# The subtraction behind a weight's low part, on GpSimd for every second piece of the first layer's weights

## The chip, the cores and the metric

The kernel runs on one core of a Trainium2 chip. A time is the device time of one execution in microseconds (us), measured on the chip; of several runs the median is given. Beside the times stands one execution that the hardware profiler recorded. The engines are TensorE (PE in the profile, PEld its weight loads), VectorE (DVE), ScalarE (ACT), GpSimd (POOL) and SyncE (SP), which issues most transfers.

## What is computed

Attention with a memory term (4 batches, 8 heads, 576 positions, 64 wide), then two feed-forward layers over 2304 tokens (512 wide, 2048 hidden). The reference, cut:

```python
scores = scale * np.matmul(q, k.transpose(0, 1, 3, 2))       # causal mask
a = softmax(scores); local = np.matmul(a, v)
q_p = phi(q)                                                   # elu + 1
mem_out = einsum(q_p, M_prev) / (einsum(q_p, z_prev) + 1e-6)
x = g * mem_out + (1 - g) * local                              # g = sigmoid(beta)
h = x @ w_in1;  r = max(h, 0);  x = (s * r * r + b) @ w_out1   # layer 1
h = x @ w_in2;  x = (h * tanh(softplus(h))) @ w_out2           # layer 2
```

## The kernel before

Every product of the two layers is made in three parts from operands that are split in two: a high part, rounded to the type that TensorE multiplies, and a low part, which is the operand less its high part. The weights come from memory as 64-bit floats, read as pairs of 32-bit words, and are turned into 32-bit floats and split on the chip.

`convert` (line 659) does this for one piece of 128 x 512 numbers. Layer 1 has 32 pieces: for each of four quarters r, four pieces j = 0 to 3 of `w_in1` and four of `w_out1` (lines 1122 and 1131). The steps of a piece, with the profile's lines:

- 673: a transfer of 512 KB brings the words (SP's queue);
- 681: the high words are scaled to floats (GpSimd for layer 1, by `C_W = 'PPPP'`);
- 685: the low words are shifted (ScalarE); 687 and 689: sign and low bits are put in (VectorE);
- 696: the high part is rounded (ScalarE, by `C_HI = 'AAAA'`);
- 699: the low part is the difference of the float and its high part; `C_LO`, one letter for each j, names its engine: D is VectorE, any other letter GpSimd.

The float lies in one of two buffers (`w32`) until line 699 has read it, and its words in one of a few raw buffers, for which the next transfers wait.

At the same time the attention runs, in halves of a head pair: `pair` (line 441) has line 506 (GpSimd), 507 (ScalarE), 508 to 512 (VectorE) for the memory term; products 542 (TensorE), row minima 552 (VectorE), exponentials 560 (ScalarE), the memory term's scaling 563 (GpSimd); the normalisation 578 (VectorE, or GpSimd for the smaller blocks of later batches) and 576 (ScalarE); transposes 601 (TensorE), copies 606 (ScalarE), products 623 (TensorE). The first four halves leave their result split in x's first block: 634 (ScalarE, high part) and 635 (VectorE, low part); 637 copies the result to a buffer `xs` of which there are two, and 639 stores it. Layer 1's first product (782) needs all four 635 steps. Until then TensorE is filled with products of zeros (1248, 100 of them). The first three blocks of layer 1 have 256 tokens (782 and 859), the next three 512; the x of the large blocks (801 to 803) is loaded into memory that becomes free when the whole attention is done (`opened`, line 1139).

The order on each engine is not written by hand. Each step is put into a `Plan` (line 176) with its engine, a planned duration, a priority and the steps that it waits for; `order` (line 230) plays this through, each engine taking the ready step of the lowest priority number, and the instructions are issued in that order. So a changed planned engine or duration (line 698: 0.6 us on VectorE, 1.23 on GpSimd) changes the order of everything after it:

```python
add(DVE if lo_dve else POOL, 0.6 if lo_dve else 1.23, prio,
    lambda: (nc.vector if lo_dve else nc.gpsimd).tensor_tensor(w_at(lo, r, j), f32(),
                                               w_at(hi, r, j).bitcast(F32), op=ALU.subtract),
```

Of the kernel before, what the change touches and what calls it, by code (L numbers as in the profile page):

```python
# [34 lines left out]
E_NORM = {True: 'DDD', False: 'PPPAD'}  # L35
E_TURN = {0: 'AAAAA', 1: 'AAAAA'}
C_HI, C_W, C2_W = 'AAAA', 'PPPP', 'AAAA'
C_LO = 'DDDD'
EARLY = 2
RAWS = (4, 4, 6, 2)  # L40

# [297 lines left out]
def attention_then_two_ffn(ctx: ExitStack, tc: tile.TileContext, qk, qz, vm, beta,  # L339
# [319 lines left out]
    def convert(layer, prio, which, r, j, raw, after=()):  # L659
# [31 lines left out]
        if layer == 1:  # L691
            hi, lo = f"w{which[0]}h", f"w{which[0]}l"
            hi_dve, lo_dve = C_HI[j] == "D", C_LO[j] == "D"
            half = Buf()
# [602 lines left out]
```

## Time and profile before

| | us |
|---|---|
| median of 3 runs | 974.88 (974.27 to 975.17) |
| the profiled execution | 973.69 |
| its span from first to last instruction | 971.9 |
| TensorE busy | 949.1 (98%) |
| VectorE busy | 672.4 (69%) |
| ScalarE busy | 641.1 (66%) |
| GpSimd busy | 190.0 (20%) |

The span leaves out 1.8 us of the profiled execution's time that lie around it. Times on the trace count from the span's start. The attention lasts until about 315 us, layer 1 until about 600, layer 2 to the end; the conversions of layer 1 run from 6 to 175 us. A line of the profile is a line of the kernel's file.

### The profile page before, as it was taken

The page shows a single profiled execution, that of the slowest core. Times are in us where ns is not written, and L with a number is a line of the kernel's source. Part 1 is how long each engine was busy: PE and PEld are TensorE (multiplying, and loading weights), DVE is VectorE, ACT ScalarE, POOL GpSimd, SP SyncE. Part 2 cuts the span into 40 slices and gives each one's busy share as a digit, 9 for nine tenths or more (in the row PEclk, how much of TensorE's full clock was granted, in tenths as well). Part 3 has the DMA queues.
Part 4 walks back from the last instruction along what each step waited for, and adds up shares of the span by engine and source line. Part 5 has one row for each costly group of instructions (what it writes and reads, how often), then busy time and mean ns, then how long its engine had stood idle before and what let it go on. Part 6 is the DMA issues. An engine that isn't in the chain of part 4 may idle for free.

```text
span 971.9 us, 18071 instructions
## 1 busy us (share of the span) xinstructions
PE 949.1 (98%) x6310; PEld 845.3 (87%) x6310; DVE 672.4 (69%) x1622; ACT 641.1 (66%) x1381; POOL 190.0 (20%) x354
## 2 busy tenths in 40 slices
PE   6899899999999999999999999999999999999998
PEld 5677688887877988888888888999999999999998
DVE  6999989777774576787212162599956799577864
ACT  4799888888887577898455575366643466344552
POOL 4643566555552000000000000000110001100100
PEclk9999999999999999999999999999999999999999
DMA  9964846656642788889400134587777657666465
GB/s 228 260 204 131 273 140 205 172 152 175 170 128 64 226 262 287 289 292 307 136 1 0 44 130 163 171 278 249 258 253 240 215 184 249 233 229 211 150 214 180
DMA packets 101995, 188.36 MB, mean 194 GB/s; under 512 B 12560, under 2 KB 76560, under 8 KB 94608
## 3 DMA queue, kind: packets, MB, share of 16 engines
q1 hardware_dynamic: 94416, 135.82, 45.6%
q0 software_dynamic: 7056, 51.38, 15.4%
q8 instruction: 50, 0.82, 0.3%
q14 instruction: 41, 0.34, 0.1%
q10 hardware_dynamic: 432, 0.01, 0.0%
HBM read 143.14 MB, written 44.04 MB: 193 GB/s over the span
## 4 chain that ended last, share of the span: by engine, by line
PE 84%; issue 6%; DMA 4%; DVE 2%; ACT 1%; POOL 1%; SPq 0%; POOLq 0%; ACTq 0%
PE bank L782 20%; PE bank L859 20%; PE bank L1000 16%; PE bank L1066 13%; PE bank L623 5%; PE bank L601 5%; PE bank L542 5%; DMA wil<-in_w_in 1%; DMA woh<-wi_split_d 1%; DMA woh<-wo_split_d 1%; DMA x_d<-xs 1%; DMA wih<-in_qz 1%; POOL Pt L563 0%; ACT Pt L560 0%; DVE stage L689 0%
## 5 line engine op out<-in xcount | busy, mean ns | idle before, releaser
L1066 PE MATMUL bank<-wol,S 128*128 128x256 f32 x828 | 111.6, 283 | 0.0
L1066 PEld LDWEIGHTS bank<-wol,S 128*128 128x128 f32 x828 | 105.3, 192 | 0.0
L981 POOL DMA_DIRECT2D wol<-wo_split_d x17 | 9.2, 541 | 469.4 <-DVE g L1006 362.2
L1000 PE MATMUL bank<-wi,woh 128*128 128x384 f32 x423 | 97.1, 335 | 0.1
L1066 PE MATMUL bank<-woh,S 128*128 128x256 f32 x684 | 93.1, 283 | 0.0
L560 ACT ACTIVATE Pt<-Pt,mx 128x64 f32<-128x64 f32 (+4 forms) x152 | 83.5, 558 | 10.1 <-DVE mx L552 9.0
L1066 PEld LDWEIGHTS bank<-woh,S 128*128 128x128 f32 x684 | 87.1, 192 | 0.0
L606 ACT COPY PT<-bank 128x384 f32<-128x384 f32 (+2 forms) x160 | 68.4, 489 | 13.7 <-PE bank L601 13.4
L1000 PEld LDWEIGHTS bank<-wi,woh 128*128 128x128 f32 x423 | 75.3, 188 | 1.1 <-DMA woh<-wi_split_d 0.3
L1000 PE MATMUL bank<-wi,wol 128*128 128x384 f32 x297 | 70.2, 334 | 0.0
L563 POOL TENSOR_SCALAR Pt<-ex,nm 128x64 f32<-128x64 f32 x152 | 58.6, 407 | 59.2 <-DVE nm L512 29.2
L601 PE MATMUL bank<-ident,Pt 128*128 128x128 f32 x444 | 61.8, 276 | 6.6 <-DVE Pt L578 4.5
L859 PE MATMUL bank<-xh,woh 128*128 128x512 f32 x240 | 64.2, 389 | 0.0
L552 DVE CUSTOM_DVE_ANT_0 Pt<-bank,mask 128x64 f32<-128x64 f32 (+3 forms) x152 | 50.2, 371 | 17.6 <-PE bank L542 10.9
L831 ACT ACTIVATE g<-bank 128x512 f32<-128x512 f32 x48 | 28.6, 596 | 50.6 <-PE bank L782 43.8
L601 PEld LDWEIGHTS bank<-ident,Pt 128*128 128x128 f32 x444 | 50.1, 141 | 9.4 <-POOL ex L506 3.7
L841 DVE TENSOR_TENSOR xh<-g,xh 128x512 fp32r<-128x512 f32 x30 | 20.7, 689 | 51.9 <-ACT xh L839 51.8
L1000 PEld LDWEIGHTS bank<-wi,wol 128*128 128x128 f32 x297 | 53.1, 188 | 0.4
L859 PEld LDWEIGHTS bank<-xh,woh 128*128 128x128 f32 x240 | 45.0, 188 | 9.0
L782 PE MATMUL bank<-yh,wi 128*128 128x512 f32 x192 | 51.0, 390 | 0.0
L782 PEld LDWEIGHTS bank<-yh,wi 128*128 128x128 f32 x192 | 35.5, 188 | 7.0
L578 POOL TENSOR_SCALAR Pt<-Pt,rs 128x64 f32<-128x64 f32 (+2 forms) x72 | 38.0, 551 | 14.9 <-DVE mx L552 9.2
(278 smaller groups left out, 2365.9 us busy)
## 6 DMA issues: line engine op xcount, KB each, us to landing
wol<-wo_split_d POOLq DMA_DIRECT2D x17, 1024.0 KB, 5.0
woh<-wo_split_d POOLq DMA_DIRECT2D x16, 1024.0 KB, 6.2
wo_split_d<-high SPq DMA_DIRECT2D x44, 256.0 KB, 3.3
stage<-in_w_in SPq DMA_DIRECT2D x21, 512.0 KB, 5.4
woh<-wi_split_d POOLq DMA_DIRECT2D x10, 1024.0 KB, 5.2
stage<-in_w_out SPq DMA_DIRECT2D x19, 512.0 KB, 4.5
stage<-wi_d SPq DMA_DIRECT2D x24, 384.0 KB, 5.1
wi_split_d<-woh SPq DMA_DIRECT2D x8, 1024.0 KB, 4.8
```

The source lines that it names most:

```text
L542: nc.tensor.matmul(ps[k][i].t[:, a:a + hi - lo], qkt(t * P, P)[rows(i)], kt(lo, hi - lo)[rows(i)], start=True, stop=True)
L552: nc.vector.tensor_tensor_reduce(at_t(i, t, D + lo, D + hi), x.t[:, a:a + hi - lo], mask[:, SP - w + lo:SP - w + hi], -SCALE, mx.t[:, i, t ...
L560: nc.scalar.activation(at_t(i, t, D, w + D), at_t(i, t, D, w + D), AF.Exp, bias=mx.t[:, i, t + k:t + k + 1], scale=-1.0, accum_out=rs.t[:, ...
L563: add(POOL, 0.33, lambda i=i, t=t: nc.gpsimd.tensor_scalar(at_t(i, t, 0, D), ex.t[:, i, t - lo_t, :], nm.t[:, i, t - lo_t:t - lo_t + 1], 1 ...
L578: (nc.vector if e == DVE else nc.gpsimd).tensor_scalar(x, x, r, *((None, ALU.mult) if e == DVE else (1.0, ALU.mult, ALU.mult)))
L601: nc.tensor.transpose(ps.t[:, x, :], at_t(i, t, c * P, (c + 1) * P), ident)
L606: (nc.vector.tensor_copy if dve else nc.scalar.copy)(PT[i].t[:, x:x + n], ps.t[:, :n])
L623: nc.tensor.matmul(pv.t[rows(i), cols].rearrange("p (t q) -> p t q", q=P), vx()[:, i, c, :], PT[i].t[:, f[0]:f[-1] + 1:f[1] - f[0] if len( ...
L782: nc.tensor.matmul(ph, w_at(nm, r, cc)[:, o:o + P], x_at(x, cc), start=(begin and part == 0 and cc == 0), stop=(part == 2 and cc == NCC - ...
L859: nc.tensor.matmul(acc[ec // per].t[:, (ec % per) * n:(ec % per + 1) * n], w_at(nm, fc // FPR, fc % FPR)[:, ec * P:(ec + 1) * P], t(x)[:, ...
L1000: nc.tensor.matmul(ps.t[:, :H2], w[i // 4].t[:, j, kk, i % 4], x[kk].t[:, k], start=begin and part == kk == 0, stop=part == 2 and kk == 1, ...
L1066: nc.tensor.matmul(acc[t].t[:, :DH], s.t[:, j, t * P:(t + 1) * P], x.t[:, k, q % 4], start=q == part == 0, stop=q == NQ2 - 1 and part == 2)
```

## The change

```diff
-C_LO = 'DDDD'
+C_LO = 'DPDP'
```

For j = 1 and j = 3, 16 of the 32 pieces, line 699 runs on GpSimd, with the same operands and result. The planned duration of these steps is 1.23 us there, so that the plan's order changes on every engine. Three places:

VectorE, about 45 us on the trace before, between the normalisation of the fourth half (578) and the fourth 635 step; `wih` is here a raw buffer of the third piece of `w_out1`. Before:

```order
L578 TENSOR_SCALAR Pt_0_494<-Pt_0_494,rs_497 128x320
L578 TENSOR_SCALAR Pt_1_495<-Pt_1_495,rs_497 128x320
L689 SCALAR_TENSOR_TENSOR stage<-stage 128x512
L687 SCALAR_TENSOR_TENSOR wih_0_320<-wih_0_320 128x512
L508 SCALAR_TENSOR_TENSOR ex_574<-wol_0_218,ex_574 128x256
L689 SCALAR_TENSOR_TENSOR stage<-stage,wih_0_320 128x512
L509 TENSOR_TENSOR wol_0_218<-ex_574,wol_0_218 128x2x128
L699 TENSOR_TENSOR wol_0_576<-stage,woh_0_518 128x512
L552 ISA Pt_0_639,mx_643<-bank_110,mask 128x448
```

With the change, the same place:

```order
L578 TENSOR_SCALAR Pt_1_494<-Pt_1_494,rs_496 128x320
L687 SCALAR_TENSOR_TENSOR stage<-stage 128x512
L508 SCALAR_TENSOR_TENSOR ex_560<-wol_0_218,ex_560 128x256
L689 SCALAR_TENSOR_TENSOR stage<-stage 128x512
L509 TENSOR_TENSOR wol_0_218<-ex_560,wol_0_218 128x2x128
L552 ISA Pt_0_638,mx_642<-bank_113,mask 128x448
L552 ISA mx_642 128x1
```

and behind the fourth 635 step, 11 rows further:

```order
L635 TENSOR_TENSOR xl_345<-bank_112,xh_336 128x256
L687 SCALAR_TENSOR_TENSOR wih_0_317<-wih_0_317 128x512
L510 TENSOR_REDUCE nm_696<-wol_0_218 128x2x2
L689 SCALAR_TENSOR_TENSOR stage<-stage,wih_0_317 128x512
L504 SCALAR_TENSOR_TENSOR rs_643<-rs_643,igate 128x2x2
```

Two things are gone ahead of the 635 step: the subtraction 699 and the pair 687 and 689 on `wih`, which now stands behind it.

GpSimd, about 29 us on the trace before. Before:

```order
L563 TENSOR_SCALAR Pt_1_326<-ex_240,nm_348 128x64
L506 TENSOR_SCALAR ex_390<-wol_0_159 128x384
L681 TENSOR_SCALAR stage<-stage 128x512
L563 TENSOR_SCALAR Pt_0_407<-ex_316,nm_419 128x64
L563 TENSOR_SCALAR Pt_1_408<-ex_316,nm_419 128x64
```

With the change:

```order
L563 TENSOR_SCALAR Pt_1_327<-ex_240,nm_338 128x64
L506 TENSOR_SCALAR ex_388<-wol_0_159 128x384
L699 TENSOR_TENSOR wi_157<-stage,wi_157 128x512
L681 TENSOR_SCALAR stage<-stage 128x512
L563 TENSOR_SCALAR Pt_0_405<-ex_320,nm_403 128x64
L563 TENSOR_SCALAR Pt_1_406<-ex_320,nm_403 128x64
```

The second moved subtraction (`w_in1`, j = 3) stands between the line-506 step of the fourth half and the scaling 681 of the next piece, ahead of the line-563 steps of the third half.

ScalarE, about 50 us on the trace before, around the fourth line-634 step. Before:

```order
L560 ACTIVATE Pt_0_639,rs_644<-Pt_0_639,mx_643 128x448
L560 ACTIVATE Pt_1_640,rs_644<-Pt_1_640,mx_643 128x448
L634 CAST xh_335<-bank_112 128x256
L685 ACTIVATE wil_0_393<-wil_0_393 128x512
L560 ACTIVATE Pt_0_641,rs_644<-Pt_0_641,mx_643 128x576
L560 ACTIVATE Pt_1_642,rs_644<-Pt_1_642,mx_643 128x576
L507 ACTIVATE ex_664<-ex_664 128x256
```

With the change:

```order
L560 ACTIVATE Pt_0_638,rs_643<-Pt_0_638,mx_642 128x448
L560 ACTIVATE Pt_1_639,rs_643<-Pt_1_639,mx_642 128x448
L507 ACTIVATE ex_664<-ex_664 128x256
L634 CAST xh_336<-bank_112 128x256
L560 ACTIVATE Pt_0_640,rs_643<-Pt_0_640,mx_642 128x576
L560 ACTIVATE Pt_1_641,rs_643<-Pt_1_641,mx_642 128x576
```

The exponential of line 507, which waits for line 506 on GpSimd, now stands ahead of line 634, not four rows behind it. Further on, in TensorE's order, 100 products stand between the attention's last product and the first of layer 1's large blocks; before it is 244.

## Rows read from the trace of the kernel before

**Rows 1.** The page's busy times: us, share of the span, instructions.
```profile
PE 949.1 (98%) x6310; PEld 845.3 (87%) x6310; DVE 672.4 (69%) x1622; ACT 641.1 (66%) x1381; POOL 190.0 (20%) x354
```
**Rows 2.** Windows: length, busy us of each engine, granted clock, DMA share, GB/s.
```profile
25.00:50.00 25.00, 21.22 (x149) 15.46 (x150) 23.91 (x91) 19.12 (x62) 17.19 (x29) 1.00 1.03 263
50.00:75.00 25.00, 24.05 (x187) 19.29 (x185) 24.60 (x72) 24.21 (x56) 10.61 (x17) 1.00 0.58 178
...
100.00:125.00 25.00, 22.43 (x180) 18.05 (x177) 23.87 (x61) 21.17 (x51) 17.12 (x23) 1.00 0.82 259
...
150.00:175.00 25.00, 25.00 (x207) 21.66 (x207) 24.17 (x67) 21.54 (x54) 16.71 (x27) 1.00 0.71 201
```
**Rows 3.** Line 699: durations in ns (least, median, longest), first and last start.
```profile
L699 DVE TENSOR_TENSOR wol<-stage,woh x16: 648/682/1077, 40.0 to 174.1; 128x512 fp32r<-128x512 f32 x16
L699 DVE TENSOR_TENSOR wi<-stage,wi x8: 650/686/1141, 10.2 to 77.3; 128x512 fp32r<-128x512 f32 x8
L699 DVE TENSOR_TENSOR wil<-stage,wih x8: 648/686/787, 104.3 to 151.6; 128x512 fp32r<-128x512 f32 x8
```
**Rows 4.** Timeline of VectorE: start, us, operation, idle before and what ended it.
```profile
15.22 1.21 DVE L689 SCALAR_TENSOR_TENSOR stage<-stage 128x512 int32<-128x512 int32 x1
...
18.45 0.68 DVE L699 TENSOR_TENSOR wi<-stage,wi 128x512 fp32r<-128x512 f32 x1
...
23.80 0.42 DVE L635 TENSOR_TENSOR xl<-bank,xh 128x256 fp32r<-128x256 f32 x1 [1.32 <-PE bank L542]
...
28.86 0.65 DVE L699 TENSOR_TENSOR wi<-stage,wi 128x512 fp32r<-128x512 f32 x1
29.43 1.86 DVE L578 TENSOR_SCALAR Pt<-Pt,rs 128x64 f32<-128x64 f32 x6
...
45.81 1.00 DVE L687 SCALAR_TENSOR_TENSOR wih<-wih 128x512 int32<-128x512 int32 x1
46.73 0.41 DVE L508 SCALAR_TENSOR_TENSOR ex<-wol,ex 128x256 f32<-128x256 f32 x1
47.07 0.72 DVE L689 SCALAR_TENSOR_TENSOR stage<-stage,wih 128x512 int32<-128x512 int32 x1
47.71 0.41 DVE L509 TENSOR_TENSOR wol<-ex,wol 128x256 f32<-128x256 f32 x1
48.80 0.69 DVE L699 TENSOR_TENSOR wol<-stage,woh 128x512 fp32r<-128x512 f32 x1 [0.67 <-ACT woh L696]
49.41 0.62 DVE L552 CUSTOM_DVE_ANT_0 Pt<-bank,mask 128x448 f32<-128x448 f32 x1
...
52.21 0.42 DVE L635 TENSOR_TENSOR xl<-bank,xh 128x256 fp32r<-128x256 f32 x1
```
**Rows 5.** Timeline of GpSimd.
```profile
6.07 0.64 POOL L681 TENSOR_SCALAR stage<-stage 128x512 f32<-128x512 f32 x1 [4.19 <-DMA stage<-in_w_in]
...
20.46 2.54 POOL L681 TENSOR_SCALAR stage<-wil 128x512 f32<-128x512 f32 x1 [3.01 <-DMA wil<-in_w_in]
...
46.25 2.56 POOL L563 TENSOR_SCALAR Pt<-ex,nm 128x64 f32<-128x64 f32 x4
48.89 1.30 POOL L506 TENSOR_SCALAR ex<-wih 128x256 f32<-128x256 f32 x1
```
**Rows 6.** Timeline of ScalarE.
```profile
46.30 0.43 ACT L637 COPY xs<-bank 128x320 f32<-128x320 f32 x1 [0.52 <-DMA x_d<-xs]
...
51.39 0.35 ACT L634 CAST xh<-bank 128x256 fp32r<-128x256 f32 x1
...
323.50 1.13 ACT L802 CAST yh<-yr 128x512 fp32r<-128x512 f32 x2
```
**Rows 7.** Timeline of TensorE.
```profile
53.79 1.22 PE L782 MATMUL bank<-xh,wi 128*128 128x256 f32 x8
...
313.11 2.17 PE L623 MATMUL bank<-PT,stage 128*64 128x256 f32 x20
...
344.58 1.09 PE L782 MATMUL bank<-yh,wi 128*128 128x512 f32 x4
```

## The prediction

> **What bounds the kernel now.** I read the busy times first [rows 1]: TensorE is busy 98% of the span, VectorE and ScalarE some two thirds, GpSimd a fifth. An average hides the stages, so the windows come next [rows 2]. From 150 us on TensorE has no idle time, so the end is the sum of its work plus whatever it stood idle before. That idle lies early: 3.78 us between 25 and 50 us, 0.95 between 50 and 75, 2.57 between 100 and 125. In the same windows VectorE is busy 23.9, 24.6 and 23.9 us of 25: while the attention and the weight conversion run together, VectorE is full and TensorE waits behind it. GpSimd has room there: 17, 11 and 17 us. The change takes work from the full engine and gives it to the one with room; its worth can only be TensorE idle time before 150 us.
>
> The moved operation [rows 3]: 32 subtractions of a 128x512 tile on VectorE, median 0.68 us, 16 of which move. On the timeline the next instruction begins 0.57 to 0.61 us after one starts, so a removed one gives VectorE 0.6 us: 16 x 0.6 = 9.6 us over 165 us.
>
> The place that counts is the first layer's first product at 53.79 us [rows 7]. It needs the four heads' first x block, whose last piece is the subtraction of line 635, at 52.21 us, the fourth of its kind [rows 4]. All TensorE work ahead of it, the filling products too, is the same in number before and after (100 fills), so what the first product gains TensorE gains.
>
> **The change part by part.** *Before the first product.* Ahead of the fourth line-635 step VectorE did lines 699 at 18.45, 28.86 and 48.80 us that are now on GpSimd, and one conversion pair (lines 687 and 689 at 45.81 and 47.07) that the plan now puts behind that step.
> - 18.45: nothing. Later VectorE stood 1.32 us idle until 23.80 for TensorE [rows 4]; what comes free is waited away there.
> - 28.86: 0.57 us, from its start to the next instruction's.
> - 48.80: 0.61 us, and the 0.67 us that VectorE waited for ScalarE just before it: 1.28.
> - The pair: 0.92 + 0.64 = 1.56 us from start to next start (busy 1.00 and 0.72). It is not saved but done later, beside layer-1 products that give TensorE other work.
>
> Together 3.4 us. Against it stand collisions. GpSimd and VectorE hinder each other on two-input steps: line 689 at 15.22 took 1.21 us where such a step takes 0.69, as GpSimd ran line 681; and line 681 on GpSimd took 2.54 us at 20.46 beside a run of VectorE steps, against 0.64 at 6.07 where VectorE was still [rows 4, 5]. I charge 0.52 us for each of the two GpSimd subtractions in this stretch: 3.4 - 2 x 0.52 = **2.4 us earlier**. ScalarE's copy of line 637 at 46.30 waited for a store to land and keeps its time; it lasts 0.43 us, and with line 634's 0.35 us [rows 6] that leaves 2.7 us for the products between before line 635 is wanted, at 52.2 - 2.4 = 49.8 us, so I don't count it as a limit. The bounds: 3.4 if there are no collisions; 0.6 if line 506 on GpSimd ends at 50.19 as now [rows 5], because ScalarE's line 507 waits for it and stands ahead of line 634 in the new order: 634 would then start at 50.8 for 51.39 [rows 6].
>
> *On GpSimd.* No row shows a two-input subtraction there. The lower bound is line 681 alone, 0.64 us, the same 512 columns with one input; the upper is the same line hindered, 2.54 us [rows 5]. I take twice the lone one, 1.3, as two inputs are twice the reading: 16 x 1.3 = 21 us more on an engine that is 42 to 69% busy in these windows [rows 2]. Behind each stand that engine's attention steps: line 563 (read by VectorE's line 578 or ScalarE's and then by the transposes), line 506, line 578 on GpSimd. Behind the first subtraction nothing is late (the next step waits for a transfer until 20.46); behind the second the next steps come later by up to 1.3 us, which GpSimd's 7.8 us of idle time in the window of 25 to 50 us take up [rows 2]. I cost these at nothing; if GpSimd's idle time were gone, each would cost the products behind it up to 1.3 us.
>
> A rule stands against that reading. The Trainium skill, page "SBUF — State Buffer", section "Who interferes with whom", says that VectorE and GpSimd share a pair of ports under an exclusive lock: whichever instruction begins first keeps it to its end, and the other is blocked fully. The 2.54 us row agrees for GpSimd as the loser. For VectorE as the loser line 687 at 45.81 agrees only in part: beside GpSimd's steps it took 1.00 us [rows 4], 0.3 over its usual time and no more. By the rule taken strictly every subtraction on GpSimd could stop VectorE for its whole length, and the sum would be that of the first rival below.
>
> *54 to 150 us.* Twelve more subtractions leave VectorE, 7.2 us, less 12 x up to 0.52. ScalarE is nearly as full as VectorE between 50 and 75 us (24.2 of 25) and keeps its work, and TensorE stands idle only 0.95 us there and 2.57 between 100 and 125 us [rows 2]. I take nothing; the bounds are 2.5 us gained (the idle time of 100 to 125 gone) and 3.6 lost (the first rival's price, below).
>
> *After 150 us.* The planner now puts more layer-1 products between attention steps, so attention ends later in TensorE's order: 100 products stand between its last product and the first of the large block, for 244. Before, those took from 315.28 to 344.58 us, 0.120 each [rows 7]; now 12.0 us. The new block's last ScalarE cast ended 9.4 us after the last attention product (323.50 + 1.13 [rows 6], less 315.28). It still fits, by 2.6 us, so nothing.
>
> The sum is -2.4 us: 973.69 - 2.4 = 971.3 for the profiled execution, whose time lies 1.2 us under the median of 974.88. On the median it is **972.5 us**.
>
> **The rivals.** *Slower: the shared port.* Each subtraction on GpSimd holds VectorE for most of its length, say 1.2 us of 1.3. It decides as soon as that hold exceeds the 0.6 us freed. Before the first product: 3.4 - 2 x 1.2 = 1.0 gained. Afterwards twelve times 1.2 - 0.6 = 7.2 us lost on a full VectorE, of which TensorE can cover about half with layer-1 products, 3.6; 974.88 - 1.0 + 3.6 = 977.5 us. For: the 1.21 and 2.54 us rows. Against: all 32 subtractions on VectorE have a median of 0.68 beside a GpSimd that is busy two fifths to two thirds of the time there [rows 2]; only two lie above 1 us [rows 3].
>
> *No difference: something else holds the first product.* Line 506 ends at 50.19 as now, or a landing does; then only 0.6 us come: 974.3 us. For: in this stretch the DMA share is 1.03 [rows 2], and ScalarE's copy at 46.30 waits for a landing [rows 6]. Against: GpSimd's 2.56 us for four line-563 steps at 46.25 [rows 5] fall beside the conversion pair, which is no longer there.
>
> *Faster still:* the relief reaches 54 to 150 us too, 2.4 + 2.5 = 4.9: 970.0 us. For: VectorE is full. Against: ScalarE is too.
>
> That the change does nothing is excluded: sixteen line-699 steps stand in GpSimd's order and are gone from VectorE's.
>
> **How the numbers follow.** My forecast 0.38, the shared port 0.25, the held first product 0.27, the larger gain 0.10. A measurement of this kernel tells about 0.2%, 1.95 us, from no change: faster is what lies under 972.9. The forecast's own range goes from 971.5 (with 3.4) to 974.3 (with 0.6), and a third of its chance, 0.13, lies above 972.9. So faster has 0.25 + 0.10 = 0.35, same 0.13 + 0.27 = 0.40, slower 0.25. The time is the likeliest case's, 972.5. The range goes down to 969.0, where both upper bounds come together (3.4 + 2.5 us), and up to 978.5, a microsecond beyond the port's 977.5, because the half that TensorE covers there is the least certain of its terms (with a third covered it is 978.7).
>
> **What would show it.** Right: line 699 on GpSimd at 1.2 to 2 us; the first line-782 product at about 51.4 us for 53.79; TensorE's idle of 25 to 50 us under 2 us; no new idle after 150 us. Wrong: line-689 and 687 steps on VectorE with a mean far above 0.75 us (the port); the first product within a microsecond of 53.8 (held); idle before the large block's first product, or transposes (line 601) waiting for GpSimd between 100 and 175 us, which would make it slower by what they wait.

## The result, and the profile after

**Slower, by 0.7%.** The changed kernel takes 981.95 us (median of 6 runs, 980.26 to 982.99), the kernel before 974.75 us beside it (6 runs): ratio 1.0069, 95% interval 1.0056 to 1.0082. A thousandth is 0.97 us, so that is 6.7 us (5.5 to 8.0); the medians lie 7.2 apart. The forecast was 972.5 us in a range of 969.0 to 978.5: the wrong sign, and beyond the range. The profiled execution took 982.99 us, 9.3 us more than the one of before; it is the longest of its six, and the one of before is shorter than any of the six beside it, so the two traces lie 2.6 us further apart than the ratio says.

The page's busy times and the windows of the changed kernel (columns as in [rows 1, 2]):

```profile
PE 954.4 (97%) x6310; PEld 850.5 (87%) x6310; DVE 677.4 (69%) x1606; ACT 640.7 (65%) x1381; POOL 207.9 (21%) x370
```

```profile
25.00:50.00 25.00, 21.89 (x156) 16.90 (x152) 23.29 (x89) 19.12 (x62) 16.41 (x30) 0.93 1.04 261
50.00:75.00 25.00, 23.30 (x183) 18.70 (x182) 24.71 (x73) 23.32 (x55) 14.25 (x18) 1.00 0.57 162
...
100.00:125.00 25.00, 21.24 (x148) 18.32 (x146) 21.16 (x47) 19.08 (x43) 17.89 (x21) 0.86 0.72 220
125.00:150.00 25.00, 22.88 (x178) 19.83 (x175) 20.49 (x55) 17.80 (x45) 15.96 (x25) 0.93 0.40 113
150.00:175.00 25.00, 24.60 (x200) 21.18 (x200) 23.77 (x60) 20.50 (x52) 16.88 (x25) 1.00 0.70 211
```

Two things stand in these lines. VectorE has 16 instructions fewer and is busy 5.0 us *more* (677.4 for 672.4). That sum alone doesn't show why: the run "order only" below, without one subtraction on GpSimd, is at 675.3. And TensorE, with the same 6310 products, is busy 5.3 us more (954.4 for 949.1): in three of these windows its granted clock is below 1.00, where the kernel before has 1.00 from 25 us on. The other 4.0 us of the 9.3 are TensorE standing idle (span less busy time: 26.8 for 22.8).

The same cut at the first layer-1 product and at 150 us, the kernel before and then the changed one:

```profile
0.00:53.79 53.79, 40.37 (x269) 30.44 (x269) 43.08 (x149) 35.48 (x104) 30.52 (x53) 0.97 0.99 248
53.79:150.00 96.21, 89.98 (x719) 73.32 (x718) 91.18 (x251) 86.54 (x210) 50.29 (x77) 1.00 0.59 184
```

```profile
0.00:53.84 53.84, 40.63 (x269) 30.96 (x269) 42.88 (x144) 35.03 (x103) 31.98 (x55) 0.94 0.99 246
53.84:150.00 96.16, 87.13 (x666) 72.73 (x665) 87.21 (x223) 79.64 (x187) 60.32 (x79) 0.95 0.54 165
```

Up to the first layer-1 product the two have done the same work in the same time. All of the 9.3 us comes behind it: TensorE stands idle 2.8 us longer until 150 us (9.0 for 6.2) and 1.4 us longer after that, and its products take 5.1 us more.

**Where the clock falls.** Windows of 5 us of the changed kernel; TensorE's busy time is the second number, the granted clock the third from the end:

```profile
30.00:35.00 5.00, 2.59 (x12) 2.19 (x13) 5.00 (x20) 2.73 (x8) 3.64 (x8) 0.80 0.94 225
35.00:40.00 5.00, 5.00 (x38) 3.76 (x37) 3.58 (x14) 4.52 (x15) 1.94 (x3) 0.86 1.06 266
110.00:115.00 5.00, 2.71 (x22) 1.74 (x16) 4.24 (x14) 4.97 (x13) 5.00 (x8) 0.99 0.87 234
115.00:120.00 5.00, 3.88 (x18) 3.88 (x19) 4.96 (x11) 2.84 (x5) 3.23 (x3) 0.50 0.99 358
...
130.00:135.00 5.00, 3.12 (x26) 2.91 (x25) 5.00 (x15) 3.87 (x14) 3.81 (x8) 1.00 0.56 167
135.00:140.00 5.00, 4.77 (x27) 4.77 (x28) 4.41 (x11) 1.95 (x4) 4.41 (x6) 0.66 0.33 108
```

Three times TensorE stands idle for 1.9 to 2.4 us of 5, and then runs for a while on the lower of its levels, 1.2 GHz (0.50). Its timeline at the same places, with the first layer-1 product ahead:

```profile
31.34 0.30 PE L601 MATMUL bank<-ident,Pt 128*128 128x128 f32 x1 [1.40 <-DVE Pt L578]
...
53.84 1.22 PE L782 MATMUL bank<-xh,wi 128*128 128x256 f32 x8
...
111.99 0.50 PE L782 MATMUL bank<-xh,wi 128*128 128x256 f32 x2 [1.00 <-ACT xh L802]
113.49 0.98 PE L782 MATMUL bank<-xh,wi 128*128 128x256 f32 x6 [0.99 <-ACT xh L802]
...
116.12 0.79 PE L782 MATMUL bank<-xl,wi 128*128 128x256 f32 x2 [1.42 <-DVE xl L803]
116.71 1.91 PE L782 MATMUL bank<-xh,wi 128*128 128x256 f32 x8
...
135.23 1.97 PE L782 MATMUL bank<-xh,wi 128*128 128x256 f32 x8 [2.12 <-DVE rt L837]
```

Eight products take 1.22 us at 53.84 and 1.91 or 1.97 behind those waits. By the granted clock of the windows of 5 us from 30 to 140 us, TensorE is on the lower level for some 13.6 us in all. Half of that, 6.8 us, bounds what the clock can cost, and the 5.3 us lie below it. The waits of 110 to 114 and of 135 us are not new, but in the kernel before they were shorter, and the clock stayed at 1.00:

```profile
110.38 0.50 PE L782 MATMUL bank<-xh,wi 128*128 128x256 f32 x2 [0.58 <-ACT xh L802]
111.88 0.98 PE L782 MATMUL bank<-xh,wi 128*128 128x256 f32 x6 [0.99 <-ACT xh L802]
...
130.15 1.22 PE L782 MATMUL bank<-xh,wi 128*128 128x256 f32 x8 [1.28 <-DVE rt L837]
```

Not every long wait brings the clock down: in the control planned with 0.58 us (below) TensorE stands 2.08 us in one piece before 91.32 us, and the granted clock is 1.00 from 85 to 100 us.

**What holds VectorE.** Line 699 on GpSimd (least, median, longest in ns), then VectorE's timeline and GpSimd's:

```profile
L699 POOL TENSOR_TENSOR wol<-stage,woh x8: 1280/1288/1398, 50.7 to 187.2; 128x512 fp32r<-128x512 f32 x8
...
L699 POOL TENSOR_TENSOR wi<-stage,wi x4: 1273/1352/1702, 17.6 to 79.4; 128x512 fp32r<-128x512 f32 x4
...
L699 POOL TENSOR_TENSOR wil<-stage,wih x4: 1260/1292/1301, 110.8 to 163.6; 128x512 fp32r<-128x512 f32 x4
```

```profile
17.23 2.48 DVE L578 TENSOR_SCALAR Pt<-Pt,rs 128x64 f32<-128x64 f32 x6
...
29.85 3.00 DVE L578 TENSOR_SCALAR Pt<-Pt,rs 128x64 f32<-128x64 f32 x6
...
50.75 0.22 DVE L552 CUSTOM_DVE_ANT_0 Pt<-bank,mask 128x64 f32<-128x64 f32 x1
...
51.12 0.75 DVE L552 CUSTOM_DVE_ANT_0 Pt<-bank,mask,mx 128x512 f32<-128x512 f32 x1
...
79.94 1.17 DVE L504 SCALAR_TENSOR_TENSOR nm<-nm,igate 128x4 f32<-128x4 f32 x1
...
90.30 0.16 DVE L504 SCALAR_TENSOR_TENSOR rs<-rs,igate 128x4 f32<-128x4 f32 x1
...
111.45 1.21 DVE L699 TENSOR_TENSOR wil<-stage,wih 128x512 fp32r<-128x512 f32 x1
112.58 0.68 DVE L803 TENSOR_TENSOR xl<-xr,xh 128x512 fp32r<-128x512 f32 x1
```

```profile
17.59 1.42 POOL L699 TENSOR_TENSOR wi<-stage,wi 128x512 fp32r<-128x512 f32 x1
...
29.87 1.27 POOL L699 TENSOR_TENSOR wi<-stage,wi 128x512 fp32r<-128x512 f32 x1
...
50.72 1.28 POOL L699 TENSOR_TENSOR wol<-stage,woh 128x512 fp32r<-128x512 f32 x1
...
79.40 1.70 POOL L699 TENSOR_TENSOR wi<-stage,wi 128x512 fp32r<-128x512 f32 x1 [1.88 <-ACT wi L696]
...
110.85 1.26 POOL L699 TENSOR_TENSOR wil<-stage,wih 128x512 fp32r<-128x512 f32 x1
112.09 1.27 POOL L563 TENSOR_SCALAR Pt<-ex,nm 128x64 f32<-128x64 f32 x1
```

Lay the two over each other. The subtraction at 29.87 ends at 31.14; the six line-578 steps that VectorE begins at 29.85 take 3.00 us, where [rows 4] has 1.86 for six, and the first transpose starts at 31.34. The 128x4 step at 79.94 takes 1.17 us, until the subtraction ends at 81.10; the same shape takes 0.16 at 90.30. The line-699 step on VectorE at 111.45 is held until 112.11 and ends 0.55 us later; and now it is GpSimd that stands: its 128x64 step at 112.09 lasts 1.27 us, until just behind the end of VectorE's line 803 at 113.26. In each of these places the one that has begun works to its end and the other stands. Not every step is hit: the line-552 steps, which read a bank of PSUM, take 0.22 and 0.75 us beside the subtraction at 50.72, as always.

Summed over the trace up to 330 us (each VectorE step less the median of its form where GpSimd was idle, put down to the GpSimd step that it overlapped most), GpSimd's subtractions cost VectorE 10.6 us, 0.66 each. The change frees 16 x 0.6 = 9.6. So in this sum VectorE isn't relieved at all.

### The profile page after: what moved, and what is told of

It reads as the page before. It is cut to its first block, busy times and chain, and to the rows that moved or that the text cites. A ratio compares the mean times of both kernels' runs of the same rounds, so it can differ in the third digit from the quotient of the medians.

```text
span 981.2 us, 18078 instructions
## 1 busy us (share of the span) xinstructions
PE 954.4 (97%) x6310; PEld 850.5 (87%) x6310; DVE 677.4 (69%) x1606; ACT 640.7 (65%) x1381; POOL 207.9 (21%) x370
## 4 chain that ended last, share of the span: by engine, by line
PE 76%; issue 4%; DMA 2%; DVE 1%; POOL 0%; ACT 0%; POOLq 0%; DVEq 0%
PE bank L859 18%; PE bank L782 18%; PE bank L1000 17%; PE bank L1066 13%; PE bank L623 4%; PE bank L601 3%; PE bank L542 3%; DMA wol<-wo_split_d 1%; DMA woh<-wi_split_d 1%; DVE stage L689 0%; PE bank L855 0%; POOL woh L981 0%; DVE nm L504 0%; POOL wol L981 0%; DVE g L1006 0%
## 5 line engine op out<-in xcount | busy, mean ns | idle before, releaser
L601 PE MATMUL bank<-ident,Pt 128*128 128x128 f32 x444 | 64.5, 283 | 9.2 <-DVE Pt L578 4.4
L601 PEld LDWEIGHTS bank<-ident,Pt 128*128 128x128 f32 x444 | 52.3, 145 | 12.1 <-POOL wi L699 2.1
```

Of the source, the lines that this page charges most:

```text
L601: nc.tensor.transpose(ps.t[:, x, :], at_t(i, t, c * P, (c + 1) * P), ident)
```

## The experiments

All of them change line 699's step for j = 1 and 3 (`add(...)` at line 698 and its lambda). Ratios are to the kernel before on the same chip, with 95% intervals; one line per run, told of one by one below.

| run | order planned as | the 16 steps | us | ratio |
|---|---|---|---|---|
| the change | the change | GpSimd subtracts | 981.95 | 1.0069 (1.0056 to 1.0082) |
| order only | the change | VectorE subtracts | 980.46 | 1.0055 (1.0038 to 1.0072) |
| three fills | the change | GpSimd, 3 fills | 977.23 | 1.0026 (1.0012 to 1.0041) |
| one fill | the change | GpSimd, 1 fill | 973.83 | 0.9990 (0.9979 to 1.0000) |
| engine only | before | GpSimd subtracts | 979.01 | 1.0045 (1.0031 to 1.0060) |
| old order, three fills | before | GpSimd, 3 fills | 974.40 | 1.0009 (1.0000 to 1.0018) |
| old order, one fill | before | GpSimd, 1 fill | 973.61 | 0.9998 (0.9989 to 1.0007) |
| quarters | the change | GpSimd, 4 pieces | 980.49 | 1.0059 (1.0044 to 1.0074) |
| charged | its own | GpSimd subtracts | 977.74 | 1.0031 (1.0020 to 1.0043) |
| charged, fills | the same | GpSimd, 3 fills | 976.87 | 1.0031 (1.0021 to 1.0041) |
| first three | its own | 3 on GpSimd | 981.80 | 1.0072 (1.0053 to 1.0091) |
| first three, fills | the same | 3 x 3 fills | 979.69 | 1.0058 (1.0042 to 1.0075) |
| other thirteen | its own | 13 on GpSimd | 981.58 | 1.0072 (1.0053 to 1.0091) |
| re-planned 0.61 | its own | VectorE subtracts | 976.69 | 1.0029 (1.0016 to 1.0041) |
| re-planned 0.58 | its own | VectorE subtracts | 978.63 | 1.0045 (1.0030 to 1.0060) |

**Order only.**

```diff
-    lambda: (nc.vector if lo_dve else nc.gpsimd).tensor_tensor(
+    lambda: nc.vector.tensor_tensor(
```

> The plan is that of the change (planned for GpSimd at 1.23 us), but all 32 subtractions are issued on VectorE. Theory A, held steps: a subtraction on GpSimd stops VectorE's tensor-tensor and tensor-scalar steps until it ends, TensorE runs dry behind them and its granted clock halves. Then this kernel has no such stops and takes 975 us (973 to 977). Theory B, the order: the plan's new order is what costs, and 980 to 983 us stay. Theory C, GpSimd late: its attention steps queue behind 21 us of subtractions; here that queue is gone: 975 us.

980.46 us, where the theories of held steps and of a late GpSimd wanted 975. So no GpSimd subtraction is needed to lose 5.4 us in this order. But it isn't the order by itself either: the next run but one has the same order and loses nothing. My reading is that the order is made for a VectorE with 9.6 us less to do, and here it has them to do after all.

**Engine only.**

```diff
-add(DVE if lo_dve else POOL, 0.6 if lo_dve else 1.23, prio,
+add(DVE, 0.6, prio,
```

> The reverse: the order is that of the kernel before (planned for VectorE at 0.6 us), but the 16 subtractions are issued on GpSimd. Theory A: 980 to 984 us, with steps such as line 504 (128x4) or 578 stretched to over 1.1 us beside a subtraction. Theory B: 975 us. Theory C: 980 us or more, but with transposes that wait for GpSimd's own lines 563, 506 and 578 rather than for VectorE.

979.01 us: in the old order, too, the engine costs 4.4 us. The same piece of VectorE's timeline and of GpSimd's, and TensorE's wait behind it:

```profile
130.39 1.06 DVE L504 SCALAR_TENSOR_TENSOR rs<-rs,igate 128x6 f32<-128x6 f32 x1
131.37 0.68 DVE L699 TENSOR_TENSOR wol<-stage,woh 128x512 fp32r<-128x512 f32 x1
131.97 0.18 DVE L581 RECIPROCAL rs<-rs 128x6 f32<-128x6 f32 x1
132.07 0.64 DVE L837 SCALAR_TENSOR_TENSOR rt<-bank,rt 128x512 f32<-128x512 f32 x1
```

```profile
130.16 1.27 POOL L699 TENSOR_TENSOR wol<-stage,woh 128x512 fp32r<-128x512 f32 x1 [0.83 <-ACT woh L696]
```

```profile
132.77 2.08 PE L782 MATMUL bank<-xh,wi 128*128 128x256 f32 x8 [2.63 <-DVE rt L837]
```

In the kernel before the same line-504 step (128x6, at 128.06 us) takes 0.16 us, and TensorE stands 1.28 us at this place. Here the step is held for 1.06, line 837 behind it comes late, TensorE stands 2.63 us, and its eight products then take 2.08 us for 1.22. VectorE is held for 13.0 us in all here.

**One fill in place of each subtraction.** These runs leave out 16 of the 32 low parts; the places and waits stay.

```diff
-    nc.gpsimd.tensor_tensor(w_at(lo, r, j), f32(), w_at(hi, r, j).bitcast(F32), op=ALU.subtract)
+    nc.gpsimd.memset(w_at(lo, r, j).bitcast(F32), 0.0)
```

> Plan and order of the change; in place of each of the 16 GpSimd subtractions GpSimd fills the 128x512 low part with zeros, so 16 of the 32 first-layer low parts are left out of the result. The waits and places are the same, but nothing is read. Theory A: if the fill doesn't stop VectorE, 9.6 us of VectorE time are free and the time is 970 to 974 us; if it does, for its own length only. Theory B: 980 to 983 us. Theory C: by the fill's length, 978 us at 0.6 us each and 982 at 1.2.

973.83 us. The first layer-1 product, and the waits that follow (TensorE's timeline; line numbers are 4 higher):

```profile
51.11 1.22 PE L786 MATMUL bank<-xh,wi 128*128 128x256 f32 x8
...
107.15 0.51 PE L786 MATMUL bank<-xh,wi 128*128 128x256 f32 x2 [1.00 <-ACT xh L806]
108.64 1.65 PE L786 MATMUL bank<-xh,wi 128*128 128x256 f32 x6 [0.98 <-ACT xh L806]
...
127.93 1.32 PE L786 MATMUL bank<-xh,wi 128*128 128x256 f32 x8 [1.93 <-DVE rt L841]
```

With the subtractions gone and nothing in their place that holds VectorE (fills cost it 0.9 us in all), the first product comes 2.7 us earlier; without collisions the forecast had 3.4. The end comes 1.0 us earlier: most of the gain is given back at 107 to 128 us, where TensorE stands 3.9 us at these three places (2.9 before) and the granted clock is 0.93 in both windows, 100 to 125 and 125 to 150 us (1.00 before). Over the two profiled executions TensorE stands 1.9 us less than before (20.9 for 22.8), and its products take 1.7 us more (950.8 for 949.1).

**Three fills**, the same with the fill made three times (1.55 us for a subtraction's 1.29):

> As the run with one fill in place of each GpSimd subtraction (973.8 us; one fill took 0.52 us), but with three fills behind each other, 1.55 us: GpSimd is occupied longer than by a subtraction (1.29 us), and nothing is read. 16 low parts are again left out of the result. Theory A, held VectorE: the fills stretch VectorE's steps little, so 973 to 976 us. Theory C, GpSimd late: its attention steps queue as behind the subtractions, 979 to 983 us.

977.23 us, between the theories. In this order GpSimd's longer occupation does cost, 1.0026 less 0.9990, 3.5 us; the subtraction costs 1.0069 less 1.0026, 4.2 us, above that, though it is shorter. The three fills hold VectorE too, but little: 2.4 us, summed in the same way as the 10.6.

**The old order with one fill, and with three:** the diff of "engine only" and the fills together.

> The order of the kernel before, and one zero fill on GpSimd (0.52 us) in place of each of the 16 subtractions; 16 low parts are left out of the result. VectorE is relieved of 16 x 0.6 us and hardly held. The prediction's relief with nothing against it: 971 to 973 us. If the time is that of the kernel before (975), the freed time is worth nothing.

> The order of the kernel before, and three zero fills on GpSimd (1.55 us) in place of each of the 16 subtractions; 16 low parts are left out. Against the run with the subtractions in the same order (979.0 us) GpSimd is occupied as long but VectorE is not held for it. Theory A: within 2 us of the run with one fill. Theory C, GpSimd late: 978 to 981 us.

973.61 and 974.40 us. Freeing VectorE of 9.6 us is worth nothing in the order of before (-0.2 us, interval -1.1 to 0.7), and occupying GpSimd for longer costs 1.1, which the intervals don't tell from nothing. The subtraction costs 1.0045 less 1.0009, 3.5 us, above that; the intervals lie apart. This is the clearest measure of the held steps: same order, same engine, a longer occupation, and only the reading taken away (VectorE is held for 2.2 us by the fills, for 13.0 by the subtractions). With the reading GpSimd's own holds go as well; no run separates them from VectorE's.

**Quarters:**

```diff
-    nc.gpsimd.tensor_tensor(w_at(lo, r, j), ...)
+    for c in range(0, 512, 128):
+        nc.gpsimd.tensor_tensor(w_at(lo, r, j)[:, c:c + 128], ...)
```

> The change with each GpSimd subtraction cut into four of 128x128. Theory A: a VectorE step waits for one piece (about 0.35 us) and not for 1.3 us, so the stops shrink to a third and the time to 976 to 979 us. Theory B: 980 to 983 us. Theory C: GpSimd is busy longer for four starts, so 982 us or more.

980.49 us, not the 976 to 979 expected. The reason stands in the durations:

```profile
L701 POOL TENSOR_TENSOR wol<-stage,woh x32: 451/458/919, 50.0 to 186.6; 128x128 fp32r<-128x128 f32 x32
```

A quarter takes 0.46 us, not 0.32, so GpSimd needs 1.83 us for a piece; the pieces still hold VectorE for 6.1 us, and line 681 now for 9.0 (7.1 in the change). I take it that what the shorter holds gave, the longer occupation took; no run separates the two, and the time isn't told from the change's.

**Charged:** the plan counts the subtraction on both engines.

```diff
     add(DVE if lo_dve else POOL, 0.6 if lo_dve else 1.23, prio, ...)
+    if not lo_dve:
+        add(DVE, 0.6, prio, lambda: None, [w, half])
```

> The change, but the plan also charges VectorE 0.6 us for each of the 16 subtractions (an empty step, nothing is issued for it), so the order is made for a VectorE that isn't relieved. Theory A with a planner misled: much of the loss is an order that counts on 9.6 us that VectorE doesn't get; 976 to 979 us. Theory A alone (the holds cost whatever the order): 980 to 983 us.

> The order of the run whose plan also charges VectorE (977.7 us), with three zero fills on GpSimd in place of each of the 16 subtractions; 16 low parts are left out. If the holds cost 4.6 us in every order: 973 us (972 to 975). If they cost nothing in an order that is made for a full VectorE: 976 to 978.

977.74 us, and with fills 976.87: the same ratio. In an order that keeps VectorE free for the length of the work that was taken from it, the held steps cost nothing that can be measured: VectorE is held for 10.7 us in the one and for 2.4 in the other, and the ratios, each known to about 0.001, are equal. What is left, 3.0 us, is this order's own together with what GpSimd's occupation costs in it; the two were not separated. Of the two times expected for the second run, 973 us missed and 976 to 978 came.

**Three alone, and the other thirteen alone:**

```diff
-hi_dve, lo_dve = C_HI[j] == "D", C_LO[j] == "D"
+hi_dve, lo_dve = C_HI[j] == "D", C_LO[j] == "D" or (which, r, j) not in (("in", 0, 1), ("in", 0, 3), ("out", 0, 1))
```

For the other thirteen `in` stands for `not in`.

> Only the three subtractions ahead of the first layer-1 product go to GpSimd (w_in1 j = 1 and 3, w_out1 j = 1 of the first quarter). The prediction's sum counted here alone: 972.5 us. Theory A: the holds take back what is freed, 974 to 977 us.

> The other thirteen alone go to GpSimd. The prediction counted them at nothing: 975 us. Theory A: the loss of the change lies here, between 60 and 190 us, 979 to 983 us, with the granted clock at half again near 115 and 135 us.

> The order of the run that moves three subtractions alone (981.8 us), with three zero fills on GpSimd (1.55 us) in place of each of the three; three low parts are left out. If the holds of three subtractions made that run slow: 975 to 977 us. If its order did: 979 to 982 us. By the holds' price so far, 4.6 us for 16, three cost about 1 us, so I expect 980 to 981.

981.80 and 981.58 us, each as much as all sixteen (7.0, 7.0 and 6.7 us): the parts don't add up, so the loss can't be placed by moving a part. The first missed both times that were expected of it, the second came as expected, with the lower clock too: in its trace, which has 0.95 elsewhere, it is 0.73 from 115 to 120 us and 0.67 from 135 to 140. With fills the first is still at 979.69: 5.7 of its 7.0 us stay without a subtraction, and the intervals overlap.

**Two controls**, with every subtraction on VectorE and only the planned duration of 16 of them changed:

```diff
-add(DVE if lo_dve else POOL, 0.6 if lo_dve else 1.23, prio,
+add(DVE, 0.6 if lo_dve else 0.61, prio,
```

> A control: all 32 subtractions stay on VectorE; only the planned duration of those of j = 1 and 3 is 0.61 us for 0.6, which makes the plan come out anew from the first of them on. Theory D, any new order: the order of the kernel before fits the chip better than most, and whatever makes the plan come out anew loses 4 to 8 us: 979 to 983 us. Theory A, held steps alone: no GpSimd subtraction, so 974 to 976 us.

> The same control with 0.58 us for 0.6, another order. Theory D: 977 to 983 us. Theory A: 973 to 976 us.

976.69 and 978.63 us: 2.8 and 4.4 us lost, with no work moved to another engine, by an order made with a hundredth or two of a microsecond in 16 steps. The first lies between the two theories; its profiled execution took 973.56 us, the least of its six, so its trace doesn't show the loss. The second came as theory D had it. Its plan puts in six more products of zeros (106, 0.17 us each), so not quite everything else is equal. Its granted clock is 1.00 from 25 to 960 us, so this order loses without the lower clock. In the second the first layer-1 product comes as early as in the run with one fill:

```profile
51.10 1.12 PE L782 MATMUL bank<-xh,wi 128*128 128x256 f32 x8
```

## Why the prediction was wrong

Two terms failed. The first is the charge of 0.52 us for each collision ahead of the first product: 2.4 us were forecast there and nothing came. The second is "I take nothing" for 54 to 150 us, which is where most of the 9.3 us between the traces were lost.

**What bounds the kernel: right, but half of it was missing.** TensorE does wait behind a full VectorE before 150 us, and most of the difference arises there. But the working took TensorE's idle time as the only price. Of the profiled execution's 9.3 us, 4.0 are idle time and 5.3 are longer products, no more than the lower clock can account for; the clock stood in no term and in none of the rivals.

**"Before the first product": the relief was right, the charge for collisions failed.** The first product came at 53.84 us for 53.79 [rows 7], not at 51.4. The relief is there: with fills it came at 51.11, and in the changed kernel the fourth line-635 step follows the third by 5.7 us (46.75 to 52.47), for 8.7 before (43.54 to 52.21). It was lost ahead of that. I charged 0.52 us for each of the two subtractions. The first turned six line-578 steps, 1.46 us in the trace of before, into 2.48, but nothing hung on it: with one fill in its place, in the same order, those steps took 1.85, and the first line-635 step came at 24.88 us in both runs. The second turned 1.86 into 3.00 (1.93 with the fill), TensorE stood 1.40 us at 31.34 and its clock fell. From there the two runs part. VectorE's second and third line-635 step with one fill, and then in the changed kernel:

```profile
36.52 0.42 DVE L635 TENSOR_TENSOR xl<-bank,xh 128x256 fp32r<-128x256 f32 x1
43.73 0.42 DVE L635 TENSOR_TENSOR xl<-bank,xh 128x256 fp32r<-128x256 f32 x1
```

```profile
39.15 0.42 DVE L635 TENSOR_TENSOR xl<-bank,xh 128x256 fp32r<-128x256 f32 x1 [0.63 <-PE bank L542]
46.75 0.42 DVE L635 TENSOR_TENSOR xl<-bank,xh 128x256 fp32r<-128x256 f32 x1
```

So one collision of the two, charged at 0.52 us, went with 2.6 us at the second of these steps and 2.7 at the first product. The size was taken from a step that met another by chance (line 689, 1.21 us for 0.69); what counts is what the plan puts behind the subtraction, and that was the normalisation for which the transposes wait.

**"What the first product gains TensorE gains": wrong.** 51.11 us with one fill gave 1.0 us at the end, and 51.10 in a control went with a loss of 4.4. A product that starts earlier meets other waits between 90 and 135 us.

**"54 to 150 us: nothing", bounds 2.5 gained or 3.6 lost: the failed term by size.** TensorE's idle time there grew by 2.8 us (9.0 for 6.2), and two of the three new stretches at the lower clock lie there, behind the waits at 112 to 116 and 135 us. In them TensorE is busy for some 9 us on the lower level, of which half, 4.5 us, is an estimate of the clock's part; with the 2.8 us that is twice the bound of 3.6.

**On GpSimd: the duration was right** (1.29 us for the 1.3 taken), **the cost of nothing was not**: in the change's order a longer occupation (three fills for one) costs 3.5 us, in the old order 1.1, not told from nothing.

**After 150 us: nearly right.** There is no idle time ahead of the large block. TensorE stands 0.4 us between 150 and 175 us, where it stood none, and one new wait of 1.0 us in layer 2, at 717 us, was not foreseen.

**The rival of the shared port named the mechanism**, and had 0.25. Its price was too low, 977.5 us: it counted the hold in VectorE's time, 1.2 us each (0.66 were measured), and left out what a wait costs TensorE and what an order costs that counts on time which doesn't come free. The signs named for it would have missed it: lines 689 and 687 have a mean of 0.80 and 0.78 us up to 190 us, not far above 0.75, because the holds fell on lines 578 and 504 too. The first product within a microsecond of 53.8 was to be the sign of another rival. The rule behind it (the Trainium skill, "SBUF — State Buffer", "Who interferes with whom") adds what I left unused: a VectorE step with two SBUF inputs contends with a GpSimd step that reads SBUF, not with one that only writes it, and reductions never contend. Here the trace agrees: lines 504, 508 and 699 were held by subtractions (0.16 to 1.17 us), the line-552 steps that read a bank were not (0.75 and 0.75), line 510's reduction was not (0.42 alone and 0.41 beside, in the run that changes the engine only), and the fills cost VectorE 0.9 us in 16. Line 578, which has one tile as its input, was held as well (1.86 to 3.00 us); the rule of two inputs doesn't cover it.

**How the 6.7 us come together.** Along the order of the change: relief -1.0, GpSimd's occupation +3.5, held steps +4.2. Along the old order: relief -0.2, occupation +1.1, held steps +3.5, and then the new order +2.3. Both end at 6.7, and neither split is the only one: the new order costs nothing where VectorE really is free (0.9990), and 5.4 us where it isn't. The 2.3 us are at the edge of the intervals, and the -0.2 and 1.1 aren't told from nothing.

**What stays open.** Why the order of the kernel before does better than every order planned anew (six in these runs; only one, with work left out, came in under it, by 0.1%) was not tried, nor whether an order could be found that does better still with the subtractions on VectorE. No version beat the kernel before: even the two that leave the work out lie within 0.1% of it.

## What to carry to other kernels

Here an operation with two SBUF inputs, given to GpSimd beside a busy VectorE, was not taken off VectorE (10.6 us held for 9.6 freed). For such a move ask which VectorE steps will fall beside it, how short they are, and which engine waits for them, and count each hold at up to the length of GpSimd's step. Where a planner sets the order, a moved operation is also a new order for everything behind it: plan the same edit with nothing moved (a hundredth of a microsecond is enough) to see what a new order alone costs, before the difference is put down to the edit. And an early product is not an early end: price TensorE's waits with the clock that follows them.

## What the runs showed of the hardware

That a 128x4 step of 0.16 us can last 1.17 us beside a GpSimd subtraction, and a GpSimd step of 0.32 us as long (1.27) beside a run of VectorE steps, was more than I had expected from the rows of before. Cut in four, a GpSimd subtraction of 1.29 us takes 4 x 0.46. And TensorE's waits of 2.1 to 2.6 us at line 782 were followed by products on the lower level of its clock (0.50), eight of them in 1.97 to 2.08 us for 1.22, while a wait of 2.08 us in another order was not.
